# Attention scores in 32x64 tiles straight from the queries, without a masked copy, and new instruction orders

## The chip, the cores and the metric

The kernel runs on one core of one Trainium2 chip. The metric is the device time of one execution in microseconds (us). An engine is named as the profile names it: PE is TensorE's matmul stream and PEld its weight loads, DVE is VectorE, ACT ScalarE, POOL GpSimd and SP SyncE, which issues transfers.

## The reference

Four layers on 2048 tokens of 448 features, attention and a gated product in turn (A, B, A, B, the weights used twice). Attention has 16 heads of 28 features; each token looks at 8 keys: itself and every second token before it.

```python
def _A_ref(x, wqkv, wo):                      # H = 16, Dh = 28
    W, dil = 8, 2
    qkv = ((x @ wqkv).reshape(B, S, 3, H, Dh)).transpose(2, 0, 3, 1, 4)
    q, k, v = qkv[0], qkv[1], qkv[2]
    idx = pos[:, None] - (jnp.arange(W) * dil)[None, :]
    mask = idx >= 0
...
    logits = jnp.einsum("bhsd,bhswd->bhsw", q, kg) * Dh ** -0.5
    logits = jnp.where(mask[None, None, :, :], logits, -1e9)
    o = jnp.einsum("bhsw,bhswd->bhsd", _softmax(logits, axis=-1), vg)
    return o.transpose(0, 2, 1, 3).reshape(B, S, D) @ wo

def _B_ref(x, w_gate, w_up, w_down):
    h = (x @ w_gate) * (x @ w_up)
    return h @ w_down

x = x + _A_ref(_layernorm(x), A_wqkv, A_wo)
x = x + _B_ref(_layernorm(x), B_w_gate, B_w_up, B_w_down)
x = x + _A_ref(_layernorm(x), A_wqkv, A_wo)
x = x + _B_ref(_layernorm(x), B_w_gate, B_w_up, B_w_down)
```

## The kernel before

Everything stays on the chip between the layers: `x_sb` holds the tokens, `xnTa` and `xnTb` their normalised transposes, `qk` the keys (plane 0) and queries (plane 1), `hT` the gated product. The even tokens come first and the odd ones behind them, two halves of 1024, so that the eight keys of a token are its neighbours in the row.

**TensorE in tiles.** A matmul can use part of the 128x128 array, and several such tiles work beside each other. The projections, the gate and up products and the down product run as pairs in two tiles of 64 rows by 128 columns (L355 in `pair`, 64 features in each). The attention uses smaller tiles. A head has 28 features, and in `qk` four heads stand on the four groups of 32 partitions. Each attention layer has nine groups of queries: the first is one block of 128 queries, the others are two blocks of 120 each. For a group, `attn_front` computes the scores of all 16 heads (the score burst, L855, into four banks of PSUM), ScalarE takes their exponent into `E_sb` (L864), VectorE masks them with a minimum (L871); `attn_back` multiplies with the values (the output burst, L889, tiles of 64 rows by 32 columns) and collects the result in a slot of `O_sb`, where it waits for its normalisation.

**The masked queries.** A score tile before has 64 rows, so it holds the keys of two heads. To keep their scores apart, VectorE writes the group's queries twice into `Qz`, once with every odd head zeroed and once with every even one (L841, `qmask`). One matmul then gives the scores of both heads, side by side. In the groups of `WIDE_S` (the first six of the first layer) the tiles are 64x64, 32 matmuls to a group; in the other twelve they are 64x32, 64 matmuls to a group, each over 64 or 80 columns. The first group of a layer has half as many.

**Strips.** A score or output burst can be cut at places given in the order, and there a step of another product is put in. That step, a pair of 64x128 matmuls, is then issued as eight strips of 64x32 (L358 in `pair`, `alt_of`): the same tile shape that output bursts and narrow score bursts have. The 64x64 bursts are not cut.

**What sets the order.** Nothing is decided at run time. `ORDER` lists for each engine the operations by number, each with the places of its cuts and the hosts of its strips, and `BANKS` gives the PSUM banks of every TensorE operation; `emit` turns dependencies into semaphore waits. Some evictions can go to ScalarE or VectorE, and `ORDER` decides which.

Of the kernel before, what the change touches and what calls it, by code (L numbers as in the profile page):

```python
# [30 lines left out]
WIDE_S = ((0, 0), (0, 1), (0, 2), (0, 3), (0, 4), (0, 5))  # L31
# [16 lines left out]
NO = 4  # L48
NE_ = 2
NR_ = 2  # L50
NZ = 1
# [46 lines left out]
def grp_nc(g):  # L98
# [21 lines left out]
    ),  # L120
    "act": (
# [224 lines left out]
def pe_cols(n):  # L346
    return n / 2.4 + 2.6
# [36 lines left out]
def build(nc, A_x, A_wqkv, A_wo, B_w_gate, B_w_up, B_w_down, out):  # L384
# [35 lines left out]
    Qz = sb([128, NZ, 2, 4, 2 * QB], bf, "Qz")  # L420
    qmask = sb([128, 2], dt.float32, "qmask")
    hT = sb([128, FC, 2, 512], bf, "hT")
    oT = sb([128, 4, HALF], bf, "oT")
# [18 lines left out]
    def one(fn, key=None):  # L442
        return [(fn, key)]
# [718 lines left out]
```

## Time and profile before

| | before |
|---|---|
| median of 3 runs | 379.52 us (379.1 to 379.61) |
| profiled execution | 380.59 us, of which the span from the first to the last instruction is 378.9 us |
| PE busy | 373.2 us (99%) |
| PEld busy | 208.2 us (55%) |
| DVE busy | 271.6 us (72%) |
| ACT busy | 199.3 us (53%) |
| POOL busy | 5.2 us (1%) |
| score bursts on PE (L855) | 912 matmuls: 736 in 64x32 tiles, 176 in 64x64 |
| output bursts on PE (L889) | 1088 matmuls in 64x32 tiles |
| strips on PE (L358) | 560 matmuls in 64x32 tiles |

A matmul's busy time is modelled: the next ones start while it is still shown as running, so neighbours overlap, and the time that a group takes is read from the start of the next group rather than from the sum of durations. A row of the order of time gives the start, the time to the last end, and the number of equal instructions.

### The profile page before, as it was taken

To read this page: it belongs to the slowest core of one execution; us is meant where nothing else is said; L and a number is where in the kernel's file an instruction comes from. 1 tells how busy PE (TensorE), PEld (TensorE's weight loads), DVE (VectorE), ACT (ScalarE), POOL (GpSimd) and SP (SyncE) were. 2 spreads that over 40 slices of the span, in tenths; PEclk is the share of its full clock that TensorE was granted. 3 is DMA by queue.
4 is the path that set the end of the run, shared out by engine and by line. 5 is a ranking of instruction groups with operands and counts; after the bars stand their busy time and mean duration, and the time that the engine had idled before them with its cause. 6 is when DMAs were issued, how large, how long until landed. Compare 5 with 4: busy or idle time off the path is not lost.

```text
span 378.9 us, 14223 instructions
## 1 busy us (share of the span) xinstructions
PE 373.2 (99%) x6372; PEld 208.2 (55%) x6372; DVE 271.6 (72%) x564; ACT 199.3 (53%) x333; POOL 5.2 (1%) x25
## 2 busy tenths in 40 slices
PE   8999999999999999999999999999999999999997
PEld 3554678544544445455766756554455454444864
DVE  6999989988786385867477978528897587275233
ACT  4898786657444565444466413556766544123310
POOL 5000000000000000000000000000000000000000
DMA  7767464610414023022102125220026104103002
GB/s 248 179 139 150 55 185 132 111 23 21 82 22 69 5 55 72 20 48 55 24 10 52 39 43 100 49 51 21 20 32 95 39 3 90 44 2 74 2 13 98
DMA packets 59892, 24.38 MB, mean 64 GB/s; under 512 B 49016, under 2 KB 59704, under 8 KB 59832
## 3 DMA queue, kind: packets, MB, share of 16 engines
q1 hardware_dynamic: 59688, 23.42, 29.0%
q8 instruction: 50, 0.82, 0.9%
q14 instruction: 10, 0.08, 0.1%
q10 hardware_dynamic: 144, 0.06, 0.1%
HBM read 9.04 MB, written 3.50 MB: 33 GB/s over the span
## 4 chain that ended last, share of the span: by engine, by line
PE 92%; ACT 4%; DMA 2%; SPq 1%; DVE 1%; issue 0%; DVEq 0%
PE ps L355 84%; PE ps L358 4%; PE ps L855 2%; ACT qk L730 2%; PE ps L889 2%; DMA hT<-in_A_wqkv_dram 2%; PE ps L1031 1%; SPq L450 1%; ACT E_sb L864 1%; ACT v_sb L822 0%; ACT R_sb L919 0%; ACT R_sb L920 0%; ACT O_sb L900 0%; DVE WQK L517 0%; DVE Qz L841 0%
## 5 line engine op out<-in xcount | busy, mean ns | idle before, releaser
L355 PE MATMUL ps<-xnTb,WGU 64*128 64x512 bf16 (+1 forms) x1902 | 171.6, 332 | 0.8 <-ACT R_sb L920 0.8
L355 PEld LDWEIGHTS ps<-xnTb,WGU 64*128 64x128 bf16 x1902 | 92.2, 94 | 70.3 <-issue 1.5
L1013 ACT ACTIVATE g_sb<-ps 128x512 bf16<-128x512 f32 x112 | 65.8, 596 | 90.7 <-PE ps L355 86.4
L1019 DVE TENSOR_TENSOR hT<-g_sb,ps 128x512 bf16<-128x512 bf16 x112 | 75.1, 681 | 40.1 <-ACT g_sb L1013 38.8
L355 PE MATMUL ps<-WD,hT 64*128 64x448 bf16 x786 | 80.5, 349 | 0.0
L980 DVE TENSOR_TENSOR x_sb<-x_sb,ps 128x448 bf16<-128x448 bf16 x62 | 36.3, 615 | 30.1 <-PE ps L355 29.8
L355 PEld LDWEIGHTS ps<-WD,hT 64*128 64x128 bf16 x786 | 37.7, 94 | 33.7 <-DVE hT L1019 0.2
L355 PE MATMUL ps<-xnTa,WQK 64*128 64x512 bf16 (+1 forms) x496 | 52.6, 353 | 0.5 <-DVE WQK L517 0.2
L864 ACT ACTIVATE E_sb<-ps,shift_sb 128x1024 bf16<-128x1024 f32 (+1 forms) x36 | 37.2, 1068 | 11.7 <-PE ps L855 11.7
L592 DVE BATCH_NORM_STATS2 st<-x_sb 128x6 f32<-128x448 bf16 x64 | 38.2, 618 | 1.4 <-DMA x_sb<-in_A_x_dram 1.2
L355 PEld LDWEIGHTS ps<-xnTa,WQK 64*128 64x128 bf16 x496 | 22.7, 94 | 22.6 <-DVE O_sb L904 1.0
L730 ACT ACTIVATE qk<-ps 128x1024 bf16<-128x1024 f32 (+1 forms) x28 | 25.4, 931 | 17.5 <-PE ps L355 17.1
L616 DVE TENSOR_SCALAR xn_sb<-x_sb,mv,rstd 128x512 bf16<-128x512 bf16 (+1 forms) x64 | 27.6, 455 | 4.9 <-ACT rstd L597 4.9
L871 DVE TENSOR_TENSOR E_sb<-E_sb,MK 128x1024 bf16<-128x1024 bf16 (+1 forms) x36 | 23.4, 658 | 9.0 <-ACT E_sb L864 8.9
L355 PE MATMUL ps<-wo_g,oT 64*128 64x448 bf16 x151 | 26.0, 350 | 0.0
L355 PE MATMUL ps<-WV,xnTa 64*128 64x336 bf16 (+3 forms) x244 | 23.6, 304 | 0.4 <-DMA WV<-in_A_wqkv_dram 0.4
L919 ACT ACTIVATE R_sb<-R_sb 128x960 f32<-128x960 f32 (+1 forms) x18 | 17.3, 961 | 11.4 <-DVE R_sb L918 11.4
L918 DVE STREAM_SHUFFLE R_sb<-O_sb 128x960 f32<-128x960 f32 (+1 forms) x18 | 21.2, 1180 | 0.0
L900 ACT ACTIVATE O_sb<-ps 128x448 f32<-128x448 f32 (+2 forms) x27 | 13.9, 548 | 11.5 <-PE ps L889 11.3
L939 DVE TENSOR_TENSOR oT<-O_sb,R_sb 128x960 bf16<-128x960 f32 (+1 forms) x16 | 17.5, 1095 | 3.2 <-ACT R_sb L920 3.2
L595 ACT ACTIVATE lnv<-mv,eps_sb 128x2 f32<-128x2 f32 (+1 forms) x33 | 9.2, 292 | 20.0 <-DVE mv L594 17.7
L920 ACT ACTIVATE R_sb<-R_sb 128x960 f32<-128x960 f32 (+1 forms) x18 | 17.3, 959 | 0.3
(67 smaller groups left out, 243.2 us busy)
## 6 DMA issues: line engine op xcount, KB each, us to landing
out_dram<-x_sb SPq DMA_DIRECT2D x15, 112.0 KB, 1.8
x_sb<-in_A_x_dram SPq DMA_DIRECT2D x3, 448.0 KB, 7.4
hT<-in_A_wqkv_dram SPq DMA_DIRECT2D x4, 224.0 KB, 5.5
WGU<-in_B_w_gate_dram SPq DMA_DIRECT2D x4, 224.0 KB, 4.1
WGU<-in_B_w_up_dram SPq DMA_DIRECT2D x4, 224.0 KB, 3.8
WD<-in_B_w_down_dram SPq DMA_DIRECT2D x2, 448.0 KB, 4.2
mv_rows<-oT SPq DMA_DIRECT2D x12, 64.0 KB, 1.7
oT<-mv_rows SPq DMA_DIRECT2D x48, 8.0 KB
```

What stands on the lines that cost most here:

```text
L355: return lambda E: E.matmul(out(), lhs(), rhs(), start=start, stop=stop)
L592: sc.add("dve", one(lambda E, B=B: E.bn_stats(st6[:, B, :], x_sb[:, B, :]), ("bn", li, B)), 525.0, deps=[("x", li - 1, B)] + ([("xn", li - ...
L616: sc.add("dve", one(lambda E, B=B, dst=dst, src=src: E.tensor_scalar(dst, src, mv[:, B, 0:1], rstd[:, B:B + 1], ALU.subtract, ALU.mult), ( ...
L730: return E.activation(dst, src, ACT.Copy) if hasattr(E, "activation") else E.tensor_copy(dst, src)
L864: return E.activation(E_sb[:, slot, 2 * hp:2 * hp + 2, 0:w], ps[:, b0:b0 + 2, 0:w], ACT.Exp, bias=shift_sb[:, 0:1], scale=SCALE)
L871: return E.tensor_tensor(e, e, MK[:, kind, 0:nc].unsqueeze(1).unsqueeze(1).to_broadcast([128, 2, w // nc, nc]), ALU.min)
L918: sc.add("dve", one(lambda E: E.stream_shuffle(R, Of, [DH] * 32), ("Rs", li, qb)), dve_est(w) + 20.0, deps=[("Oa", li, g)] + prev, prio=prio)
L919: sc.add("act", one(lambda E: E.activation(R, R, ACT.Ln), ("Rl", li, qb)), act_est(w, False), deps=[("Rs", li, qb)], prio=prio)
L939: return E.tensor_tensor(dst, O.rearrange("p d h n -> p h d n"), Rv.rearrange("p d h n -> p h d n"), ALU.mult)
L980: sc.add("dve", one(lambda E: E.tensor_tensor(x_sb[:, B, :], x_sb[:, B, :], ps[:, bk[w], 0:D], ALU.add), ("x", li, B)), dve_est(D), deps=[ ...
L1013: sc.add("act", one(lambda E, gs=gs, bk=bk: E.activation(g_sb[:, gs, :], ps[:, bk[0], :], ACT.Copy), ("G", li, j, f0)), act_est(512), deps ...
L1019: return E.tensor_tensor(hT[:, f0:f0 + nf, hs, 0:nt], v(g_sb[:, gs, :]), v(ps[:, bk[1], :]), ALU.mult)
```

## The change

The score tile becomes 32 rows by 64 columns. Each matmul takes the 28 rows of one head, unmasked, from `qk`: 64 keys against 64 queries. The four heads of a row group pattern go to four PSUM banks, and eight tiles (four groups of rows, two of columns) can work at once. All groups have this form, `WIDE_S` is gone, and with it `Qz`, `qmask` and the 36 masking instructions. A group of two blocks now has 64 matmuls in every case, of 64 columns each. `E_sb` is laid out by head, which changes the addresses that the minimum and the output burst read; the group that lies across the two halves takes its minimum in two parts. `O_sb` gets six slots for four.

```diff
-WIDE_S = ((0, 0), (0, 1), (0, 2), (0, 3), (0, 4), (0, 5))
+SCORES = "C32"
-NO = 4
+NO = 6
-NZ = 1
...
 ORDER = {
     "pe": (
-        "41 42 43 44 45 46 47 48 49 50 51 52 53 54 112 115 55 56 57 58 211 130 212 133 139 241 136 242 205 235 206 236 229 201 230 203 231 202 157 232 199 154 "
+        "39 40 41 42 43 44 45 46 47 48 49 50 51 52 110 113 53 54 55 56 209 128 131 210 134 238 137 239 199 203 200 204 232 226 233 155 228 227 152 229 201 197 "
...
-        zs, zprev = ring("z", ("S", li, qbs[-1]))
-        def fz(E, a):
-            return E.tensor_scalar(Qz[:, zs, a, :, 0:end - tok], qk[:, 1, :, tok:end], qmask[:, a:a + 1], None, ALU.mult)
-        sc.add("dve", [((lambda E, a=a: fz(E, a)), ("Qz", li, g) if a else None) for a in range(2)], 2 * (4 * (end - tok) * 0.33 + 62.0), deps=qdeps + [zprev, "c_qm"], prio=prio)
...
-        wide = (li, g) in WIDE_S
-        KN = 64 if wide else 32
-        for hc, d, c, s_, p in [(hc, d, c, s_, p) for hc in range(4) for d in range(nd) for s_ in range(64 // KN) for c in range(2) for p in range(2)]:
+        for hc, d, c, r in [(hc, d, c, r) for hc in range(4) for d in range(nd) for c in range(2) for r in range(4)]:
             ck, nk, cq, nq = qb_info(qbs[d])
-            ks, qs = ck + 64 * c + KN * s_, cq + 56 * c - tok
-            b, h = e_at(nd, hc, d, p)
-            lo, hi = max(0, ks - qs - tok), min(nc, ks - qs - tok + KN + W)
-            ins.append((lambda E, hc=hc, c=c, s_=s_, p=p, b=b, h=h, ks=ks, qs=qs, lo=lo, hi=hi: E.matmul(
-                ps[64 * c + KN * s_:64 * c + KN * s_ + KN, bk[b], 2 * nc * h:2 * nc * (h + 1)].rearrange("p (a n) -> p a n", a=2)[:, :, lo:hi], qk[64 * p:64 * p + 64, 0, hc, ks:ks + KN],
-                Qz[64 * p:64 * p + 64, zs, :, hc, qs + lo:qs + hi], start=True, stop=True, tile_position=(64 * p, 64 * c + KN * s_)), None))
+            ks, qs, o = ck + 64 * c, cq + 56 * c, (d * 4 + hc) * nc
+            lo, hi = max(0, ks - qs), min(nc, ks - qs + 64 + W)
+            ins.append((lambda E, hc=hc, c=c, r=r, ks=ks, qs=qs, o=o, lo=lo, hi=hi: E.matmul(
+                ps[64 * c:64 * c + 64, bk[r], o + lo:o + hi], qk[32 * r:32 * r + DH, 0, hc, ks:ks + 64], qk[32 * r:32 * r + DH, 1, hc, qs + lo:qs + hi],
+                start=True, stop=True, tile_position=(32 * r, 64 * c)), None))
...
-        sc.add("pe", ins, sum(pe_cols(2 * n) for n in cols) / (4 if wide else 8), deps=deps + [prev, ("Qz", li, g)], mode="C64" if wide else BURST, acquire=bk, prio=prio)
+        sc.add("pe", ins, sum(pe_cols(n) for n in cols) / 8, deps=deps + [prev], mode=SCORES, acquire=bk, prio=prio)
...
-            sc.add("dve", one(fm, ("E", li, g, hp)), dve_est(2 * w, 2.0, 60.0), deps=[("Ex", li, g, hp), f"c_mk{kind}"], prio=prio)
+            sc.add("dve", [((lambda E, hp=hp, p=p: fm(E, hp, *p)), ("E", li, g, hp) if p is parts[-1] else None) for p in parts], dve_est(2 * w, 2.0, 60.0 * len(parts)),
+                   deps=[("Ex", li, g, hp)] + [f"c_mk{k}" for k in sorted(set(kinds))], prio=prio)
```

The strips keep their shape. After the change ten of the 18 score bursts are cut, nine of them three times and one twice; before, ten were cut, three times each. In the changed kernel L354 stands for L355, L357 for L358, L838 for L855, L873 for L889.

First place: PE, the ninth group of the first layer, whose score burst is cut in both kernels by strips of the gate and up products. `32x2x40` is an output of 32 partitions and 80 columns (a 64x32 tile with two heads), `64x64` one of 64 partitions (a 32x64 tile). Before:

```order
L855 MATMUL ps<-Qz,qk 32x2x32 x2
L855 MATMUL ps<-Qz,qk 32x2x40 x4
L855 MATMUL ps<-Qz,qk 32x2x32 x4
L855 MATMUL ps<-Qz,qk 32x2x40 x4
L855 MATMUL ps<-Qz,qk 32x2x32 x2
L358 MATMUL ps<-xnTb,WGU 32x512 x8
L855 MATMUL ps<-Qz,qk 32x2x32 x2
```

And after the change:

```order
L838 MATMUL ps<-qk 64x64 x16
L357 MATMUL ps<-xnTb,WGU 32x512 x8
L838 MATMUL ps<-qk 64x64 x16
L357 MATMUL ps<-xnTb,WGU 32x512 x8
L838 MATMUL ps<-qk 64x64 x8
L357 MATMUL ps<-xnTb,WGU 32x512 x8
L838 MATMUL ps<-qk 64x64 x24
```

The cuts stand after the same numbers of matmuls (16, 16 and 8), and the strips between them have another tile shape than the scores now.

Second place: PE, early in the first layer, where score bursts stand whole between projections. Before, the third group:

```order
L889 MATMUL ps<-E_sb,v_sb 32x64 x64
L355 MATMUL ps<-xnTa,WQK 128x512 x42
L855 MATMUL ps<-Qz,qk 64x128 x32
L355 MATMUL ps<-xnTa,WQK 128x256 x14
L355 MATMUL ps<-xnTa,WQK 128x512 x6
```

After the change:

```order
L354 MATMUL ps<-xnTa,WQK 128x256 x6
L354 MATMUL ps<-xnTa,WQK 128x512 x8
L354 MATMUL ps<-xnTa,WQK 128x256 x8
L838 MATMUL ps<-qk 64x64 x64
L354 MATMUL ps<-wo_g,oT 128x448 x8
```

Where 32 matmuls of 128 columns stood are 64 of 64 columns.

Third place: DVE at the same stage, with the eviction of queries and keys (L730, then L725), the mask copies (L841) and the minimum (L871, then L855). Before:

```order
L841 TENSOR_SCALAR Qz<-qk,qmask 128x960 x2
L795 CAST v_sb<-ps 128x8x28
L939 TENSOR_TENSOR oT<-O_sb,R_sb 128x4x128
L904 TENSOR_TENSOR O_sb<-O_sb,ps 128x8x8
L918 STREAM_SHUFFLE R_sb<-O_sb 128x960
L730 CAST qk<-ps 128x2x512 x2
```

After the change:

```order
L790 CAST v_sb<-ps 128x8x28
L923 TENSOR_TENSOR oT<-O_sb,R_sb 128x4x128
L884 COPY O_sb<-ps 128x8x56
L888 TENSOR_TENSOR O_sb<-O_sb,ps 128x8x8
L902 STREAM_SHUFFLE R_sb<-O_sb 128x960
L725 CAST qk<-ps 128x2x512
```

The mask copies are gone, and an eviction of outputs (L884) that ScalarE did stands in their stead. Over the whole program VectorE now does 12 evictions of queries and keys instead of 8 and 14 of outputs instead of 9, and ScalarE as many fewer.

More of the change, by code (lines that the diff above doesn't have):

```diff
@@ L503, in build @@
     memset("pool", ones32, 1.0, "c_ones", 100)
-    sc.add("dve", one(lambda E: E.memset(qmask[:], 0.0), "i_qm"), 60, prio=-39.5)
-    sc.add("dve", [((lambda E, r=r: E.memset(qmask[32 * r:32 * r + DH, r % 2:r % 2 + 1], 1.0)), "c_qm" if r == 3 else None) for r in range(4)], 240, deps=["i_qm"], prio=-39.5)
     wb = Banks(1)
@@ L562, in build @@
     WO = [("wp", w, b) for w in range(2) for b in range(4)] + [("wp", 2, 0), ("wp", 2, 1)] + [("wo", j) for j in range(4)]
[L564 removed]
+    rings = {n: [None] * k for n, k in (("xn", NXN), ("o", NO), ("v", NV), ("v2", NV2), ("e", NE if PAIRED else 2 * NE), ("r", NR), ("g", NG))}
     rpos = {n: 0 for n in rings}
@@ L836, in attn_front @@
         k0, tok, end = qb_info(qbs[0])[0], qb_info(qbs[0])[2], sum(qb_info(qbs[-1])[2:])
-        qdeps = [("QK", li, j, c) for j in chunks_of(li, tok, end) for c in range(4)]
         deps = [("QK", li, j, c) for j in chunks_of(li, k0, end) for c in range(4)]
-        zs, zprev = ring("z", ("S", li, qbs[-1]))
-        def fz(E, a):
-            return E.tensor_scalar(Qz[:, zs, a, :, 0:end - tok], qk[:, 1, :, tok:end], qmask[:, a:a + 1], None, ALU.mult)
-        sc.add("dve", [((lambda E, a=a: fz(E, a)), ("Qz", li, g) if a else None) for a in range(2)], 2 * (4 * (end - tok) * 0.33 + 62.0), deps=qdeps + [zprev, "c_qm"], prio=prio)
         slot, prev = ring("e", ("AV", li, qbs[-1]))
@@ L866, in attn_front, with fm @@
         for hp in range(2):
[L867 to L872 removed]
+            kinds = [0 if q == 0 else 2 if q == STRADDLE else 1 for q in qbs]
+            parts = [(0, nd, kinds[0])] if len(set(kinds)) == 1 else [(d, d + 1, kinds[d]) for d in range(nd)]
+            def fm(E, hp, a, z, kind):
+                e = E_sb[:, slot, 2 * hp:2 * hp + 2, 4 * a * nc:4 * z * nc].rearrange("p b (m n) -> p b m n", n=nc)
+                return E.tensor_tensor(e, e, MK[:, kind, 0:nc].unsqueeze(1).unsqueeze(1).to_broadcast([128, 2, 4 * (z - a), nc]), ALU.min)
+            sc.add("dve", [((lambda E, hp=hp, p=p: fm(E, hp, *p)), ("E", li, g, hp) if p is parts[-1] else None) for p in parts], dve_est(2 * w, 2.0, 60.0 * len(parts)),
+                   deps=[("Ex", li, g, hp)] + [f"c_mk{k}" for k in sorted(set(kinds))], prio=prio)
         return slot
@@ L886, in attn_back @@
             vw = v_sb[64 * c:64 * c + 64, vslot[q], 32 * h:32 * h + 32] if t < 0 else v2_sb[64 * c:64 * c + 64, v2slot[q], 32 * t:32 * t + 32]
-            eb, eh = e_at(nd, hc, d, b // 2)
-            eo = (2 * eh + b % 2) * nc
-            ins.append((lambda E, b=b, c=c, o=o, vw=vw, eb=eb, eo=eo: E.matmul(ps[32 * b:32 * b + 32, bk[c], o:o + nc], vw, E_sb[64 * c:64 * c + 64, slot, eb, eo:eo + nc],
+            eo = (d * 4 + hc) * nc
+            ins.append((lambda E, b=b, c=c, o=o, vw=vw, eo=eo: E.matmul(ps[32 * b:32 * b + 32, bk[c], o:o + nc], vw, E_sb[64 * c:64 * c + 64, slot, b, eo:eo + nc],
                                                                start=True, stop=True, tile_position=(64 * c, 32 * b)), None))
```

10 lines of the change are left out of this document (removed), and 112 rows, old and new, of tables (BANKS, ORDER).

## The prediction

> **What bounds the kernel now.** I read the page first, then the busy time by stretch, then the waits of TensorE, and last the order of time inside single bursts.
>
> ```profile
> PE 373.2 (99%) x6372; PEld 208.2 (55%) x6372; DVE 271.6 (72%) x564; ACT 199.3 (53%) x333; POOL 5.2 (1%) x25
> PE   8999999999999999999999999999999999999997
> PE 92%; ACT 4%; DMA 2%; SPq 1%; DVE 1%; issue 0%; DVEq 0%
> ```
>
> TensorE is busy in every slice, and 92% of the chain that ended last is its own. A busy PE need not be at its peak, so the next views ask whether it ever stands still.
>
> ```profile
> 0.00:20.00 20.00, 18.09 (x204) 9.42 (x206) 16.65 (x59) 12.86 (x30) 5.20 (x25) 1.00 0.73 203
> 20.00:60.00 40.00, 38.73 (x846) 24.60 (x844) 36.60 (x80) 34.67 (x53) 0.00 (x0) 1.00 0.64 143
> 60.00:300.00 240.00, 239.93 (x4420) 131.77 (x4416) 178.92 (x355) 128.57 (x209) 0.00 (x0) 1.00 0.25 48
> ...
> PE ps L509 <- DVE hT L480: 1.2, 1, 1.2
> PE ps L355 <- ACT R_sb L920: 0.8, 1, 0.8
> PE ps L355 <- DMA WV<-in_A_wqkv_dram: 0.4, 1, 0.4
> PE ps L355 <- DVE WQK L517: 0.2, 1, 0.2
> ```
>
> The stretches list time, then PE, PEld, DVE, ACT and POOL busy, the granted clock (1.00 throughout) and DMA. From 60 to 300 us TensorE has 0.07 us of idle time in 240, while VectorE and ScalarE have 61 and 111 us to spare. There, a nanosecond added to TensorE's stream is a nanosecond of the kernel, and one taken from VectorE is nothing. Only from 20 to 60 us do three engines share the limit: PE 38.73, DVE 36.60, ACT 34.67 of 40. So the change is priced on TensorE, burst by burst.
>
> **The change on TensorE: what a burst costs now.** Here is the order of time on PE around four bursts, then the means by shape (rows of lines by form; "64*32" is tile rows by tile columns).
>
> ```profile
> 23.67 0.59 PE L355 MATMUL ps<-xnTa,WQK 64*128 64x512 bf16 x4
> 24.20 0.64 PE L855 MATMUL ps<-Qz,qk 64*64 64x128 bf16 x32
> 24.77 0.60 PE L355 MATMUL ps<-xnTa,WQK 64*128 64x512 bf16 x3
> ...
> 80.06 0.59 PE L355 MATMUL ps<-xnTb,WGU 64*128 64x512 bf16 x4
> 80.59 0.25 PE L889 MATMUL ps<-E_sb,v_sb 64*32 64x64 bf16 x16
> 80.66 0.40 PE L358 MATMUL ps<-xnTb,WGU 64*32 64x512 bf16 x8
> 80.87 0.24 PE L889 MATMUL ps<-E_sb,v_sb 64*32 64x64 bf16 x16
> 80.93 0.40 PE L358 MATMUL ps<-xnTb,WGU 64*32 64x512 bf16 x8
> 81.14 0.21 PE L889 MATMUL ps<-E_sb,v_sb 64*32 64x64 bf16 x8
> 81.17 0.40 PE L358 MATMUL ps<-xnTb,WGU 64*32 64x512 bf16 x8
> 81.39 0.27 PE L889 MATMUL ps<-E_sb,v_sb 64*32 64x64 bf16 x24
> 81.59 0.39 PE L355 MATMUL ps<-xnTb,WGU 64*128 64x512 bf16 x2
> ...
> 117.88 0.26 PE L855 MATMUL ps<-Qz,qk 64*32 64x64 bf16 x16
> ...
> 118.94 0.60 PE L355 MATMUL ps<-xnTb,WGU 64*128 64x512 bf16 x4
> ...
> 197.99 0.68 PE L855 MATMUL ps<-Qz,qk 64*32 64x64 bf16 x64
> 198.60 0.61 PE L355 MATMUL ps<-xnTb,WGU 64*128 64x256 bf16 x8
> ```
>
> ```profile
> L355 PE MATMUL ps<-xnTa,WQK 64*128 64x512 bf16 x384 | 46.4, 377 | 0.2
> L355 PE MATMUL ps<-WD,hT 64*128 64x448 bf16 x786 | 80.5, 349 | 0.0
> L855 PE MATMUL ps<-Qz,qk 64*64 64x128 bf16 x168 | 3.6, 219 | 0.0
> ```
>
> *Price of a change of tile shape.* The four big matmuls at 80.06 are two pairs. A single one lasts 0.377, so the second pair started 0.59 - 0.377 = 0.21 us after the first; that is the time a pair streams. Two pairs take 0.43, yet the short burst begins 0.53 after 80.06: 0.10 us is lost at the change from 64x128 tiles to 64x32. At 23.67 the change to 64x64 costs the same (24.20 - 23.67 - 0.43). On the way out, the last of the 32 matmuls started at 24.20 + 0.64 - 0.219 = 24.62 and streams about 0.05 (32 of them, four at a time, in 0.42); the next pair comes at 24.77: 0.10 again.
>
> *No change of shape, no price.* Strips (L358, big matmuls cut into 64x32 tiles) and the short matmuls of the attention outputs have one shape. A round of eight strips takes 80.87 - 80.66 = 0.21 and 81.39 - 81.17 = 0.22 us, which is what a pair of the same columns takes uncut. Strips inside a burst are free.
>
> *What the new order adds.* The changed scores use 32x64 tiles; the strips stay at 64x32. Ten of the 18 score bursts are cut by strips, nine of them three times and one twice: 29 cuts. Before, all cuts were within one shape. Now each is a change in and a change out, 58 in all. Outside the cuts there were 70 changes (68 between big matmuls and bursts, two where an output burst met a score burst of 64x64 directly) and are now 71 (70 and one). With two more at the program's ends the count goes from 72 to 131: 59 more. At 0.10 us: **+5.9 us**. No row shows 32x64 meeting 64x32. The bounds are 0 (the strip rounds above) and 0.10. I take 0.10, since in this program every meeting of two shapes pays it, whether the columns alone change (64x128 to 64x32 and to 64x64) or the rows alone. For the rows, the end of the program:
>
> ```profile
> 370.31 0.73 PE L355 MATMUL ps<-WD,hT 64*128 64x448 bf16 x6
> 370.97 0.55 PE L1031 MATMUL ps<-WD,hT 128*128 128x448 bf16 x2
> ```
>
> Three pairs of 448 columns begin 0.19 us apart ((0.73 - 0.35)/2, by the 0.35 us that one such matmul lasts), the third at 370.69; it streams until 370.88, and the 128x128 tile comes at 370.97: 0.09 us. A change of both is nearer to these than to no change.
>
> [...]
>
> *The bursts themselves.* Less their exit (0.10), an uncut group of 32 at 64x64 takes 24.77 - 24.20 - 0.10 = 0.47; an uncut group of 64 at 64x32 takes 198.60 - 197.99 - 0.10 = 0.51; a cut score burst, less three rounds of strips, 118.94 - 117.88 - 0.65 - 0.10 = 0.31; a cut output burst, whose 64 matmuls have the 64 columns that the new scores have, 81.59 - 80.59 - 0.65 - 0.10 = 0.25 (0.65 is three rounds at 0.216). Before: 5 x 0.47 + 10 x 0.31 + 0.51, and the two groups of half size taken at half (0.24 and 0.26): 6.5 us. After: 6 x 0.51 + 10 x 0.25, and two halves at 0.26: 6.1 us. **-0.4 us**. Half the columns per matmul in the wide groups buys nothing, because there are twice as many matmuls.
>
> *Weight loads.* They double to 64 columns, all hidden behind the stream in my sum:
>
> ```profile
> L855 PEld LDWEIGHTS ps<-Qz,qk 64*32 64x32 bf16 x736 | 9.2, 90 | 5.8 <-issue 2.9 <-DVE hT L1019 0.9 <-DVE xn_sb L616 0.4
> L855 PEld LDWEIGHTS ps<-Qz,qk 64*64 64x64 bf16 x176 | 2.7, 106 | 2.0 <-issue 0.8 <-ACT rstd L597 0.6 <-ACT g_sb L1013 0.4
> ```
>
> A load of 64 columns is 16 ns longer than one of 32, and eight run beside each other. If the cover is gone, a tile may take a new load only as fast as the wide groups show, every 0.47/8 = 0.059 us instead of the 0.031 of a round at 0.25/8: 80 rounds x 0.028 = +2.2 us. This is a rival below.
>
> **The change on the other engines.**
>
> ```profile
> L841 DVE TENSOR_SCALAR Qz<-qk,qmask 128x960 bf16<-128x960 bf16 x32 | 13.5, 464 | 2.5 <-ACT qk L730 2.5
> L841 DVE TENSOR_SCALAR Qz<-qk,qmask 128x512 bf16<-128x512 bf16 x4 | 1.2, 353 | 0.3 <-ACT qk L730 0.3
> L730 ACT ACTIVATE qk<-ps 128x1024 bf16<-128x1024 f32 x22 | 22.2, 1022 | 17.3 <-PE ps L355 17.1
> L730 DVE CAST qk<-ps 128x1024 bf16<-128x1024 f32 x6 | 7.3, 1214 | 0.0
> ...
> 48.60 0.64 PE L855 MATMUL ps<-Qz,qk 64*64 64x128 bf16 x32
> 50.05 0.40 PE L355 MATMUL ps<-xnTb,WGU 64*128 64x256 bf16 x4 [0.81 <-ACT R_sb L920]
> ```
>
> The masked copies, 14.7 us of VectorE, go, and the new order hands VectorE evictions that ScalarE did (two more 1024-wide QK evictions at 1.21 us against 1.02 on ScalarE, five more of the attention outputs). From 60 us on both are covered by TensorE: nothing. Before that, the front is worth something: the burst at 48.60 is followed after 1.45 us where its like took 0.57, a wait of 0.88 us, and PE's idle time from 20 to 60 us is 1.27. The bounds are 0 and -2 us (that idle, and some more under modelled ends); lighter ScalarE and VectorE should take part of it, and the scores no longer wait for a mask (0.93 us for a group's two). I take **-0.8 us**. What is late next there is the QK eviction itself, which the scores still need. The masking minimum is split in two for the group that straddles the two token halves (four instructions more over the two layers, on VectorE, covered as above). Two more slots for outputs let an output burst start before older ones are normalised; no row of TensorE's waits names such a slot, so nothing. The queue of SP issues the same transfers in another order, and the chain names none of them between 20 us and the last output.
>
> **The sum**: 5.9 - 0.4 - 0.8 = +4.7 us. The profiled execution took 380.59 us for a span of 378.9, so it should become a span of 383.6 and 385.3 us. The median of the runs is 379.52, lower by 1.07; on it the forecast is **384.2 us**.
>
> **Rivals.**
>
> *No drain between 32x64 and 64x32 tiles.* Then the 5.9 us fall to the 0.1 of one change and the change is worth -0.4 - 0.8: 378.3 us, from 377.3 to 379.3. For it speaks that strips and short matmuls of one shape flow without a gap; against it stand the three pairs of shapes above, each with its 0.09 to 0.10. It decides as soon as a change costs under 1.2/59 = 0.020 us.
>
> *Weight loads come through.* 384.2 + 2.2 = 386.4 us. For it: the scores' loads are twice as wide and each tile gets one every 0.03 us, which no row shows; against it, 16 ns more of duration is little. [...]
>
> *Cheaper changes or a fuller gain in front.* A change at 0.06 us, or all 2 us of the front's waits: 381 to 382.5 us.
>
> **How the numbers follow.** Full drain, 382.5 to 386: 0.64. Weight loads on top, 386 to 388: 0.08. The cheaper case, 380.5 to 382.5: 0.10. No drain: 0.18, of which 0.11 lies under 378.76. A change within 0.2% (378.76 to 380.28) is about what a measurement of this kernel cannot tell from none. So faster 0.11, same 0.07, slower 0.82. The range from 380.5 to 387.5 holds the first three but for the end of the second, 0.81.
>
> **What would show it.** In the changed kernel's order of time, strips should begin 0.09 to 0.10 us later than the stream of the scores ahead of them allows, and scores the same after strips; a round of strips inside a score burst should take 0.31 us, not 0.21, with the outputs' bursts as before. PE's idle time from 60 to 300 us stays near nothing while the span grows. If the rounds inside score bursts stay at 0.21, the forecast is wrong and the first rival right; if eight scores take 0.06, the second.

## The result: 389.88 us, slower, and by twice what was forecast

| | before | after |
|---|---|---|
| median | 379.4 us (379.1 to 379.61, 4 runs) | 389.88 us (389.76 to 390.49, 4 runs) |
| ratio to before | | 1.028, 95% interval 1.0262 to 1.0298 |
| profiled execution, its span | 380.59 us, 378.9 us | 390.49 us, 388.8 us |

The direction was right and the size was not: +4.7 us was forecast, +10.5 came by the medians (+9.9 between the two profiled executions), and 389.88 lies above the range. The page of the changed kernel, its busy engines and its chain:

```profile
PE 381.6 (98%) x6518; PEld 209.7 (54%) x6518; DVE 266.2 (68%) x536; ACT 194.8 (50%) x324; POOL 5.1 (1%) x25
PE 94%; ACT 2%; DMA 2%; DVE 1%; issue 1%; DVEq 0%
```

TensorE is still the chain. Its busy time grew by 8.4 us, while VectorE lost 5.4, which bought nothing. The same stretches as before the change, and TensorE's longest waits:

```profile
20.00:60.00 40.00, 37.42 (x996) 23.45 (x994) 32.32 (x66) 32.77 (x48) 0.00 (x0) 1.00 0.55 126
60.00:300.00 240.00, 239.03 (x4236) 129.43 (x4232) 170.38 (x335) 119.37 (x196) 0.00 (x0) 1.00 0.26 48
...
PE ps L354 <- DMA xnTb<-xn_sb: 1.6, 1, 1.6
PE ps L504 <- DVE hT L477: 1.2, 1, 1.2
PE ps L354 <- issue: 0.9, 1, 0.9
```

From 20 to 60 us PE is busy for 37.42 us instead of 38.73: the lighter VectorE and ScalarE (32.32 and 32.77 busy, from 36.60 and 34.67) did not become less waiting but more. From 60 to 300 us there is almost 1 us of idle time where there was 0.07, and it is one wait, put down to "issue", which is to say to nothing that the profile shows. The clock is 1.00 throughout.

The order of time on PE in a cut score burst, the counterpart of the burst at 117.88 before:

```profile
121.70 0.27 PE L838 MATMUL ps<-qk 28*64 28x64 bf16 x16
121.90 0.41 PE L357 MATMUL ps<-xnTb,WGU 64*32 64x512 bf16 x8
122.24 0.27 PE L838 MATMUL ps<-qk 28*64 28x64 bf16 x16
122.43 0.41 PE L357 MATMUL ps<-xnTb,WGU 64*32 64x512 bf16 x8
122.77 0.23 PE L838 MATMUL ps<-qk 28*64 28x64 bf16 x8
122.94 0.41 PE L357 MATMUL ps<-xnTb,WGU 64*32 64x512 bf16 x8
123.28 0.30 PE L838 MATMUL ps<-qk 28*64 28x64 bf16 x24
123.51 0.60 PE L354 MATMUL ps<-xnTb,WGU 64*128 64x512 bf16 x4
...
204.07 0.71 PE L838 MATMUL ps<-qk 28*64 28x64 bf16 x64
204.71 0.94 PE L354 MATMUL ps<-xnTb,WGU 64*128 64x256 bf16 x14
```

(The profile writes the 32x64 tile as 28*64, by the 28 rows that are used.) A round of eight strips inside a score burst takes 122.24 - 121.90 = 0.34 us, where it took 0.21, and sixteen scores ahead of strips take 0.20 instead of 0.07. The whole burst lasts 123.51 - 121.70 = 1.81 us, of which three rounds of strips stream 0.64 (at the pace of uncut pairs, 0.213 us for 512 columns): 1.17 us for the scores. Before, the burst at 117.88 took 118.94 - 117.88 - 0.64 = 0.42.

To see where all of the time is, I took the start of every matmul from the traces and counted each burst so, from its first matmul to the next big one, less its strips' own stream (a wait begins where the next matmul would have started):

| us | score bursts | output bursts | waits of PE | rest | first to last matmul |
|---|---|---|---|---|---|
| before | 8.45 | 7.72 | 3.44 | 355.36 | 374.97 |
| after | 15.80 | 7.95 | 5.38 | 355.73 | 384.86 |
| difference | +7.35 | +0.23 | +1.94 | +0.37 | +9.89 |

The split depends a little on where a wait is taken to begin. With the idle time of PE that the profile shows as the waits (3.24 and 4.80 us), the four differences are +7.50, +0.27, +1.56 and +0.56.

So two things are to be explained: score bursts that cost 7.35 us more (forecast: +5.5), and waits that cost 1.94 us more (forecast: 0.8 less). The theory for the first is the forecast's, a price for each change of tile shape, dearer than 0.10; its rivals are the width of the weight loads, the rows of the tile as such, and the number of short matmuls in a row. For the second it is the new order, or something that the profile does not name.

### The profile page after: what moved, and what is told of

The parts are those of the page before. It is cut to its first block, busy times and chain, and to the rows that moved or that the text cites. A ratio compares the mean times of both kernels' runs of the same rounds, so it can differ in the third digit from the quotient of the medians.

```text
span 388.8 us, 14482 instructions
## 1 busy us (share of the span) xinstructions
PE 381.6 (98%) x6518; PEld 209.7 (54%) x6518; DVE 266.2 (68%) x536; ACT 194.8 (50%) x324; POOL 5.1 (1%) x25
## 4 chain that ended last, share of the span: by engine, by line
PE 94%; ACT 2%; DMA 2%; DVE 1%; issue 1%; DVEq 0%
PE ps L354 82%; PE ps L357 4%; PE ps L838 3%; PE ps L504 2%; DMA xnTb<-xn_sb 2%; PE ps L873 2%; PE ps L1015 1%; ACT qk L725 1%; PE ps L630 0%; DVE R_sb L902 0%; DVE oT L923 0%; ACT R_sb L904 0%; ACT R_sb L903 0%; ACT O_sb L884 0%; DVE O_sb L884 0%
## 5 line engine op out<-in xcount | busy, mean ns | idle before, releaser
L354 PE MATMUL ps<-xnTb,WGU 64*128 64x512 bf16 (+1 forms) x1908 | 172.1, 332 | 1.6 <-DMA xnTb<-xn_sb 1.6
L354 PEld LDWEIGHTS ps<-xnTb,WGU 64*128 64x128 bf16 x1908 | 92.3, 94 | 71.1 <-issue 2.5
L1003 DVE TENSOR_TENSOR hT<-g_sb,ps 128x512 bf16<-128x512 bf16 x112 | 75.5, 681 | 54.5 <-ACT g_sb L997 52.7
L354 PE MATMUL ps<-WD,hT 64*128 64x448 bf16 x790 | 80.6, 349 | 0.9 <-issue 0.9
L354 PEld LDWEIGHTS ps<-WD,hT 64*128 64x128 bf16 x790 | 38.2, 94 | 35.0 <-issue 1.7
L354 PE MATMUL ps<-xnTa,WQK 64*128 64x512 bf16 (+1 forms) x496 | 52.0, 352 | 0.4 <-DVE WQK L520 0.2
L354 PEld LDWEIGHTS ps<-xnTa,WQK 64*128 64x128 bf16 x496 | 23.2, 94 | 22.4 <-DVE xnTa L640 1.0
L855 DVE TENSOR_TENSOR E_sb<-E_sb,MK 128x1024 bf16<-128x1024 bf16 (+2 forms) x40 | 23.6, 606 | 7.0 <-ACT E_sb L847 7.0
L725 ACT ACTIVATE qk<-ps 128x1024 bf16<-128x1024 f32 (+1 forms) x24 | 22.5, 948 | 11.3 <-PE ps L354 11.0
L354 PE MATMUL ps<-wo_g,oT 64*128 64x448 bf16 x154 | 26.3, 350 | 0.4 <-DVE oT L923 0.4
L354 PE MATMUL ps<-WV,xnTa 64*128 64x336 bf16 (+3 forms) x242 | 23.6, 305 | 0.0
L884 ACT ACTIVATE O_sb<-ps 128x512 f32<-128x512 f32 (+3 forms) x22 | 11.5, 557 | 13.5 <-PE ps L873 13.5
L838 PEld LDWEIGHTS ps<-qk 28*64 28x64 bf16 x1088 | 10.2, 103 | 12.6 <-issue 9.6
```

Source lines behind the costliest of these rows:

```text
L354: return lambda E: E.matmul(out(), lhs(), rhs(), start=start, stop=stop)
L725: return E.activation(dst, src, ACT.Copy) if hasattr(E, "activation") else E.tensor_copy(dst, src)
L838: ins.append((lambda E, hc=hc, c=c, r=r, ks=ks, qs=qs, o=o, lo=lo, hi=hi: E.matmul(ps[64 * c:64 * c + 64, bk[r], o + lo:o + hi], qk[32 * r ...
L855: return E.tensor_tensor(e, e, MK[:, kind, 0:nc].unsqueeze(1).unsqueeze(1).to_broadcast([128, 2, 4 * (z - a), nc]), ALU.min)
L1003: return E.tensor_tensor(hT[:, f0:f0 + nf, hs, 0:nt], v(g_sb[:, gs, :]), v(ps[:, bk[1], :]), ALU.mult)
```

## Experiments

All times are medians, and all ratios are to the kernel before on the same chip (379.5 to 380.3 us).

**1. No cuts in the score bursts.** The changed kernel; the hosts of the strips follow their burst whole.

```diff
-495*3.5/468:1+311:1
+495 468 311
-543*2.4.5/405:3
+543 405
... (and eight more)
```

> The changed kernel with no cut in a score burst: the ten cut bursts stand whole and their strips are issued as ordinary pairs behind them; all else as changed. Theory A (58 changes of tile shape at the cuts cost about 0.125 us each): a cut burst takes 1.16 us beside its strips, a whole one 0.64, so ten of them give 5.2 us back: 389.9 - 5.2 = 384.7 us, with the waits outside the bursts as in the changed kernel. Rival B (the new score tiles are slow in themselves, by their weight loads or the new places of the operations, and the cuts cost no more than strips of the old shape did): less than 1.5 us back, 388.4 us or more.

385.19 us (384.59 to 386.17), ratio 1.0098 (1.0065 to 1.0132): theory A's size. Without any cut the 58 changes are gone, and the score bursts fall from 15.80 to 10.87 us.

```profile
119.94 0.72 PE L826 MATMUL ps<-qk 28*64 28x64 bf16 x64
120.59 1.69 PE L342 MATMUL ps<-xnTb,WGU 64*128 64x512 bf16 x14
```

An uncut burst takes 0.65 us (0.64 as a mean), so the scores alone, with no strips between, cost more than a cut burst of before, 0.42. The gain from the cuts' removal is 15.80 - 10.87 = 4.93 us over 58 changes, 0.085 each: less than the 0.125 that theory A gives a change, so something is lost with the cuts; experiment 5 shows what.

**2. The new tile shape in the old order.** The kernel before, its masked copies still made but not read; the scores come from `qk` in 32x64 tiles as in the changed kernel.

```diff
-            b, h = e_at(nd, hc, d, p)
-                Qz[64 * p:64 * p + 64, zs, :, hc, qs + lo:qs + hi], ..., tile_position=(64 * p, 64 * c + KN * s_)), None))
+                ps[64 * c:64 * c + 64, bk[r], o + lo:o + hi], qk[32 * r:32 * r + DH, 0, hc, ks:ks + 64], qk[32 * r:32 * r + DH, 1, hc, qs + lo:qs + hi],
+                start=True, stop=True, tile_position=(32 * r, 64 * c)), None))
```

> The kernel before, its orders, its four output slots and its masked copies (still written, now read by nobody), with the new score tiles alone: 32x64, straight from the queries. Theory A: 30 cuts, 60 changes of shape at 0.125 = 7.5 us, and five whole groups at 0.64 for 0.57 us: 379.4 + 7.5 + 0.4 = 387.3 us; the waits stay at the 3.4 us of the kernel before. Rival C (at least half of the loss comes with the new orders, not with the tiles): 384 us or less.

392.23 us (390.56 to 393.47), ratio 1.028 (1.023 to 1.0331): slower than expected. Its cut bursts take 1.17 us like those of the changed kernel, so the shape and not the order makes the price. What comes on top is not in the bursts' changes but in stops, and most of it in one place:

```profile
48.77 0.59 PE L853 MATMUL ps<-qk 28*64 28x64 bf16 x47
51.06 0.34 PE L853 MATMUL ps<-qk 28*64 28x64 bf16 x17 [1.70 <-issue]
```

TensorE stops in the middle of a score burst, 17 matmuls from its end, and waits for nothing that the profile names. Two shorter stops of the same kind stand at 24.94 (0.65 us) and at 208.24 (0.39). Experiment 7 takes them up, and the last section what follows the longest.

**3. The old tile shape in the new order.** The changed kernel with score tiles of 64 rows by 32 columns, straight from the unmasked queries.

```diff
-                ps[64 * c:64 * c + 64, bk[r], o + lo:o + hi], qk[32 * r:32 * r + DH, 0, hc, ks:ks + 64], qk[32 * r:32 * r + DH, 1, hc, qs + lo:qs + hi],
-                start=True, stop=True, tile_position=(32 * r, 64 * c)), None))
+                qk[64 * p:64 * p + 64, 0, hc, ks:ks + 32],
+                qk[64 * p:64 * p + 64, 1, hc, qs + lo:qs + hi].unsqueeze(1).to_broadcast([64, 2, hi - lo]), start=True, stop=True, tile_position=(64 * p, 64 * c + 32 * s_)), None))
```

> The changed kernel, its orders and six slots, with score tiles of 64 rows by 32 columns again, but without a mask: the scores of two heads are mixed, which the time does not see. Left out: the masking. Theory A: no change of shape at a cut, 58 x 0.125 = 7.3 us less: 382.6 us; what stays above the 379.4 before are waits of the new orders, about 2 us, and some 0.5 us of whole bursts. Rival C: the loss is with the orders, 385 us or more. If even the front's waits go, 380.5 us or less.

384.32 us (381.74 to 385.75), ratio 1.0086 (1.0059 to 1.0113): 5.6 us less than the changed kernel with the same orders and no masks, and the ratio is lower by 1.9 points. As a time it lies between theory A's 382.6 and rival C's 385; PE stands idle for 5.48 us here, more than in the changed kernel (4.80), and part of that is in stops of experiment 7's kind. The bursts decide. The one that stands at 121.70 there, first and last rows:

```profile
121.06 0.26 PE L839 MATMUL ps<-qk 64*32 64x64 bf16 x16
121.13 0.41 PE L357 MATMUL ps<-xnTb,WGU 64*32 64x512 bf16 x8
121.34 0.26 PE L839 MATMUL ps<-qk 64*32 64x64 bf16 x14
...
121.86 0.32 PE L839 MATMUL ps<-qk 64*32 64x64 bf16 x24
122.11 1.04 PE L354 MATMUL ps<-xnTb,WGU 64*128 64x512 bf16 x8
```

0.21 us for a round of strips and 1.05 for the burst, as before. The same cuts at the same places are free where the shapes agree; with 32x64 tiles they cost 1.168 - 0.414 = 0.754 us, over six changes 0.126 each. The orders, the cuts and the strips are the same in both; the scores differ in tile shape, and with it in weights loaded (32 columns instead of 64) and in columns streamed (64 to 80 instead of 64). Standing whole, the two shapes cost nearly the same (0.615 and 0.64 us), so it is the meeting with the strips that makes the price.

**4. No masked copies.** The kernel before with the mask copies shrunk to one column; the scores mix two heads.

```diff
-            return E.tensor_scalar(Qz[:, zs, a, :, 0:end - tok], qk[:, 1, :, tok:end], qmask[:, a:a + 1], None, ALU.mult)
+            return E.tensor_scalar(Qz[:, zs, a, 0, 0:1], qk[:, 1, 0, tok:tok + 1], qmask[:, a:a + 1], None, ALU.mult)
...
-                Qz[64 * p:64 * p + 64, zs, :, hc, qs + lo:qs + hi], ...
+                qk[64 * p:64 * p + 64, 1, hc, tok + qs + lo:tok + qs + hi].unsqueeze(1).to_broadcast([64, 2, hi - lo]), ...
```

> The kernel before with its orders and tiles, but the masked copies shrunk to one column and the scores read from the unmasked queries: heads are mixed, the time of 14.5 us of VectorE is left out. The forecast had put 0.8 us on a lighter front: 378.6 us. Theory D (VectorE's work is covered nearly everywhere, and what the front waits for is not VectorE): 379.0 to 379.5 us.

379.76 us (378.77 to 381.09), ratio 0.9977 (0.9955 to 1.0). VectorE's 14.7 us of masks are worth at most 0.45% of the time. In the trace PE's idle time falls from 3.24 to 2.54 us, but all except 0.1 us of that lies in the first 20 us, ahead of the first masked copy (at 20.67 us in the kernel before). From 20 to 60 us, where the forecast had looked for its gain, the idle time goes from 1.27 to 1.18 us.

**5. One cut instead of three.** The changed kernel.

```diff
-495*3.5/468:1+311:1
+495*4/468:1 311
-543*2.4.5/405:3
+543*4/405:1
... (and eight more)
```

> The changed kernel with a single cut in each of its ten cut score bursts instead of three or two: 10 strip rounds stay, 20 of the 58 changes between scores and strips. Theory A (a cut costs two changes of shape, 0.25 us together, and gives part of it back, since an uninterrupted run of short matmuls slows down after the first rounds): a burst less its strips' own stream takes about 0.64 us, as uncut (0.638), against 1.17 with three cuts; the sum of score bursts comes to about 11 us, as without any cut (10.87), and the time to 385 us. Theory B (only the number of changes counts, at 0.126 each, and an uncut burst's 0.64 is a burst's own work): 0.64 + 0.25 = 0.89 us a burst, score bursts about 13.4 us, and 387.5 us.

386.56 us (385.33 to 388.13), ratio 1.0175 (1.0143 to 1.0207). The span of the profiled run, 383.6 us, is 0.8 longer than without cuts; the medians differ by 1.4, so the time alone lies between the theories' 385 and 387.5. The bursts tell them apart:

```profile
120.16 0.33 PE L826 MATMUL ps<-qk 28*64 28x64 bf16 x32
120.42 0.42 PE L345 MATMUL ps<-xnTb,WGU 64*32 64x512 bf16 x8
120.77 0.33 PE L826 MATMUL ps<-qk 28*64 28x64 bf16 x32
121.03 1.04 PE L342 MATMUL ps<-xnTb,WGU 64*128 64x512 bf16 x8
```

121.03 - 120.16 - 0.21 = 0.66 us a burst (0.659 to 0.677 over the ten): theory A of the two, against 0.89 by theory B. The first cut costs two changes and gives back nearly as much. The reason shows in the pieces: 32 matmuls up to the strips take 0.26 us with the change in it, but 64 in one go take 0.65; a long run of short matmuls slows down after its first rounds, in both shapes. In an uncut burst the first four rounds of eight start within 0.12 us, the fifth 0.12 us after the fourth, and the later ones 0.067 us apart; a piece between two strips is too short to get there. (Before, the 64 of 64x32 at 197.99 take 0.61 uncut and 0.41 cut three times.) So cuts by strips are worth about 0.2 us to a burst, and this worth was part of every cut before. Why a long run slows down no run shows.

**6. The price of a change by itself.** The kernel before; the fourth of the seven steps of 84 products is issued as eight strips. (Twelve of the 84 are halves of the down product, with 448 columns instead of 512.)

```diff
+                elif e == "pe" and len(got) == 1 and got[0].alt and len(got[0].alt) > 3 and got[0].acquire is not None and got[0].acquire.kind == 1 and len(got[0].ins) == 14:
+                    o = got[0]
+                    seq = [(o, n) for n in range(6)] + [(o, o.alt[3][q]) for q in range(8)] + [(o, n) for n in range(8, 14)]
```

> The kernel before, with the fourth of the seven steps of 84 gate and up products (512 columns, the ones that host no strips) issued as eight strips of 64x32 instead of a pair of 64x128: 168 more changes of tile shape, each between matmuls of 512 columns, with no short matmul near. Theory A (the drain alone is 0.094 to 0.103 us, and the rest of the 0.126 found per change in the score bursts comes from the short matmuls' own first rounds): +16 to +17 us, 396 us. Theory B (a change costs 0.126 us whatever stands on its sides): +21 us, 400.6 us. Theory C (strips themselves, hidden so far, cost nothing and a drain is partly covered by 512 columns): under +14 us.

399.04 us (398.91 to 400.26), ratio 1.05 (1.047 to 1.053): +19.5 us for 168 changes, 0.116 each, between theory A (0.10) and theory B (0.126).

```profile
150.50 0.73 PE L358 MATMUL ps<-WD,hT 64*128 64x448 bf16 x6
151.16 0.38 PE L361 MATMUL ps<-WD,hT 64*32 64x448 bf16 x8
151.48 0.74 PE L358 MATMUL ps<-WD,hT 64*128 64x448 bf16 x6
```

Three pairs of 448 columns stream 0.56 us and the strips come after 0.66; the strips stream 0.187 and the next pair comes after 0.32. Over all 84 places, alike within 3 ns: about 93 ns on the way into the strips and 128 on the way out, from the first strip, as the eight strips start over 23 ns and the next pair comes 105 ns later than the stream of the last of them alone would ask. The pair behind that is some 10 ns late as well. A round of strips costs 0.227 to 0.231 us in all, by the pace that is given to an uncut pair; 0.227 is used below. The forecast took the way out to be as dear as the way in and left the 23 ns out. The remaining 0.126 - 0.1135 = 0.012 per change goes with the short matmuls themselves: the first round of eight scores after strips takes 52 ns, the next ones 32, and 20 ns to two changes is near it.

**7. Another 112 instructions ahead of everything.** The changed kernel; eight warm-up matmuls as eight of 64 columns each.

```diff
-    ... one(lambda E, n=n: E.matmul(ps[:, n % NBK if n < NBK else wb[0], :], warm[:, 0:128], warm, start=True, stop=True), ("warm", n)), 427.0
+    return lambda E: E.matmul(ps[:, n % NBK if n < NBK else wb[0], 64 * i:64 * i + 64], warm[:, 0:128], warm[:, 64 * i:64 * i + 64], start=True, stop=True)
+    ... [(fw(n, i), ("warm", n) if i == 7 else None) for i in range(8)] if n < 8 else one(...)
```

> The changed kernel with eight of its warm-up matmuls, which compute nothing that is used, issued as eight of 64 columns each instead of one of 512: 112 more instructions on TensorE ahead of all work, the same order behind. Theory A (TensorE's unexplained idle times, 1.07 us near 70.7 in the changed kernel and 1.9 near 49 in the version with the orders of before, are waits for the next 256 instructions of 64 bytes, whose count in the trace is 193 more than a multiple of 256): the idle time near 70.7 goes from that matmul, and whatever idle time of PE over 0.3 us is put down to nothing lies where the recounted number of instructions is again 193 more than a multiple of 256; the time falls by up to 1 us or, if another boundary meets dense work, stays. Theory B (the idle time belongs to that matmul, a wait the profile does not show): it stays at the same matmul, 112 instructions later in the count.

392.31 us (391.14 to 392.92), ratio 1.032 (1.0294 to 1.0345): not faster, slower. But the places tell the theories apart. In the changed kernel, around the wait for "issue", and at the same work here:

```profile
70.35 0.73 PE L354 MATMUL ps<-WD,hT 64*128 64x448 bf16 x5
71.98 0.91 PE L354 MATMUL ps<-WD,hT 64*128 64x448 bf16 x7 [0.90 <-issue]
```

```profile
72.57 1.30 PE L354 MATMUL ps<-WD,hT 64*128 64x448 bf16 x12
...
52.26 1.15 PE L354 MATMUL ps<-xnTb,WGU 64*128 64x256 bf16 x18
54.71 0.39 PE L354 MATMUL ps<-xnTb,WGU 64*128 64x256 bf16 x4 [1.31 <-issue]
```

The twelve matmuls of the down product now run through, and a new wait of 1.31 us has come up inside a gate and up product that ran through before. (The time is not these stops alone: a wait of 1.21 us for ScalarE's eviction of values at 69.61 is new, and the wait of 1.57 us for `xnTb` is gone, since `xnTb` landed at 49.11 us instead of 49.88. PE's idle time is 6.02 us in all, against 4.80.) Counting all of PE's records (matmuls, weight loads, and the semaphore waits that no view counts as busy) up to each stop over half a microsecond from start to start that is put down to "issue":

| kernel | records up to the stop | stop, from start to start | remainder by 256 |
|---|---|---|---|
| after | 3009 | 1.25 us | 193 |
| 2 (shape, old order) | 705, 1985, 7617 | 0.85, 1.91, 0.58 | 193, 193, 193 |
| 3 (64x32, new order) | 705, 3009, 7617 | 0.71, 1.42, 0.53 | 193, 193, 193 |
| 5 (one cut) | 705, 3009, 7361 | 0.63, 0.92, 0.60 | 193, 193, 193 |
| 7 (112 more) | 961, 2241, 7617 | 0.81, 1.57, 0.85 | 193, 193, 193 |
| 9 (below) | 705 | 0.70 | 193 |
| 1, 3, 5, at one place near 48.5 us | 1883, 1887, 1883 | 0.68, 0.71, 0.73 | 91, 95, 91 |
| before, 4, 6, 8 | none | | |

Fourteen stand at the same place of a 256-instruction piece, and the place in the work moved with the 112 instructions. The other three are a kind of their own: they stand in the last matmuls of the output burst just ahead of the wait for `xnTb`, 7 to 11 records before it; their cause is open, and as the product behind them waits for `xnTb` anyway, they cost little. The transfers agree: queue q8 moved 51 pieces of 16 KB in the changed kernel's run (the row lists pieces, MB and share).

```profile
q8 instruction: 51, 0.84, 0.9%
```

In the changed kernel one ran from 69.30 to 70.54 us, and the stop is from 70.73 to 71.98; in this one, from 52.11 to 53.23 and from 53.14 to 54.71. With 13,171 records in all, 51 pieces are one for each 256. The traces also tell when such a stop comes. Number the places with remainder 193 and the pieces in order: the second place goes with the first piece, and so on. All fourteen stops end 1.25 to 1.65 us after their piece has landed. At the 521 places of the eleven traces that TensorE reaches 1.7 us or more after the landing, no matmul comes over 0.32 us behind the one before it. (Fifteen other places within 1.65 us have a shorter stop or none.) In the kernel before the shortest such distance is 1.75 us, and it has no stop. How many pieces TensorE holds at a time no run shows. Most pieces come in time (50 of 51 in the changed kernel, all in the one before), and why some come late is open: the stops stand in or shortly behind bursts, but other pieces that are used up as fast come in time. So theory A holds, with its less welcome end: a shift moves the stops and does not remove them.

**8. The burst back ahead of the wait, first form.** In the changed kernel's order the score burst of the eighth pair of blocks had moved behind the gate and up product that waits for `xnTb`. Here it goes back.

```diff
-... 337 346 289 358 292 ...
+... 337 346 358 289 292 ...
```

> The changed kernel with one move in its order: the score burst of the first layer's eighth pair of blocks goes ahead of the gate and up product that waits for xnTb (near 48 us), where before had it; PSUM banks of seven operations are renamed for it, and one exponent on ScalarE goes ahead of one eviction. Theory A (the transposed tokens come at the same time, 50.0 to 50.2 us, whatever TensorE does before, so the burst fills the wait): the idle time there falls from 1.6 to about 0.9 us and the time by 0.6 to 0.8 us, to 389.2. Theory B (the wait follows the burst, because ScalarE or VectorE then have more to do ahead of the transpose's source): no change, 389.9 us.

391.45 us (389.16 to 393.19), ratio 1.0292 (1.0258 to 1.0327): inconclusive, because the renamed banks made waits of their own, and the runs fall into two groups. Four have a mean granted clock of 0.995 or 0.996 and take 391.4 to 393.19 us; two have 1.00 and take 389.16 and 389.25 (the last section shows two traces with such a drop).

```profile
48.13 0.68 PE L873 MATMUL ps<-E_sb,v_sb 64*32 64x64 bf16 x64 [0.41 <-ACT qk L725]
48.73 1.04 PE L838 MATMUL ps<-qk 28*64 28x64 bf16 x64
50.83 1.38 PE L354 MATMUL ps<-xnTb,WGU 64*128 64x256 bf16 x22 [1.05 <-DVE v_sb L817]
```

The product now waits for VectorE's eviction of values from the bank that it was given, and the output burst for an eviction of keys. These two waits are 1.46 us, nearly the 1.57 that the move was to shorten. That the profiled run still meets theory A's 389.2 is luck: it has no stop for instructions near 70.7, and the move was not made for that.

**9. The same move without these waits.** The banks of all later operations are exchanged in a ring, and VectorE evicts the values first.

```diff
-... 337 346 289 358 292 ...   (pe)
+... 337 346 358 289 292 ...
-... 525 348 349 338 275 ...   (dve)
+... 525 338 348 349 275 ...
-289:45 292:67 ... 358:0123 ...   (banks; all later ones likewise, 01 to 23, 23 to 45, 45 to 67, 67 to 01)
+289:67 292:01 ... 358:2345 ...
```

> The changed kernel with the same move as in e5_front (the score burst of the eighth pair of blocks ahead of the gate and up product that waits near 48 us), now without new waits of its own: the PSUM banks of everything from there on are exchanged in a ring, so that the output burst and the product keep banks that are free as early as in the changed kernel, and VectorE evicts the values ahead of the two instructions on the outputs. Theory A (the product waits for xnTb alone, which comes at 49.9 to 50.2 us whatever TensorE does before): the wait ahead of the product falls from 1.46 us to about 0.85, as in before, and the time by 0.6 us, to 389.2, unless a wait for instructions arises elsewhere, since 256-instruction pieces now end at other work. Theory B (the wait follows the burst): the product starts 0.6 us later, the time stays at 389.9.

392.09 us (391.15 to 392.44), ratio 1.0315 (1.0293 to 1.0337): right at its place and wrong in the time. The place first, in the changed kernel and here:

```profile
47.97 0.68 PE L873 MATMUL ps<-E_sb,v_sb 64*32 64x64 bf16 x64
50.22 1.71 PE L354 MATMUL ps<-xnTb,WGU 64*128 64x256 bf16 x28 [1.57 <-DMA xnTb<-xn_sb]
```

```profile
48.17 0.68 PE L873 MATMUL ps<-E_sb,v_sb 64*32 64x64 bf16 x64
48.78 1.06 PE L838 MATMUL ps<-qk 28*64 28x64 bf16 x64
50.09 3.23 PE L354 MATMUL ps<-xnTb,WGU 64*128 64x256 bf16 x56 [0.24 <-DVE O_sb L884]
...
62.56 0.94 PE L354 MATMUL ps<-wo_g,oT 64*128 64x448 bf16 x8
65.77 0.28 PE L873 MATMUL ps<-E_sb,v_sb 64*32 64x64 bf16 x24 [2.28 <-DVE st L587]
```

The product starts at 50.09 instead of 50.22 with the whole burst done ahead of it; the wait fell from 1.57 to 0.24 us. `xnTb` lands at 49.84 us here and at 49.88 in the changed kernel, so the move left its arrival alone (theory A). Thirteen microseconds later an output burst waits 2.28 us, where the changed kernel had no wait, and that takes all of it back, with slower matmuls behind it (last section). The instruction named there is statistics of another layer's tokens, on which the burst does not depend. Of what it does depend on, the transposed values come late: the transfer issued at 60.21 us lands at 65.68, and the burst's first weights are loaded at 65.74. In the changed kernel the same transfer was issued at 59.15 and landed at 62.55, ahead of the burst at 64.33. That fits a wait for it, but no run was made to test it. The number of records there, 2562, is 2 more than a multiple of 256, so it is not one of the stops at remainder 193.

## Why the forecast was right in direction and wrong in size

*The drain.* Shown as a price: strips inside 32x64 scores pay, 0.126 us a change, strips inside 64x32 scores in the same order do not (experiment 3), and strips between big matmuls pay too, 0.1135 us a change (experiment 6). So the rival without a drain falls. In the prediction and the expectations the word stands for the time that a change takes, which is what the runs show; what TensorE does in that time they do not show.

*The count.* 59 more changes was right: the matmuls' shapes in the traces change 72 times before and 131 times after.

*The price of a change, 0.10 us: the first step that failed.* It was read as the same in and out. Alone it is 0.1135 (experiment 6), in the score bursts 0.126 (experiment 3). For the 58 changes at the cuts that is 58 x 0.126 = 7.3 us instead of 5.8.

*The bursts themselves, -0.4 us: failed.* A cut score burst was given the 0.25 us of a cut output burst (the one at 80.59, among the shortest: 0.37 us with its exit, where most take 0.39). Without its changes it measures 1.168 - 3 x 0.227 - 0.105 = 0.38 (0.105 for the exit). Part of that is the 0.012 per change above. The halves and whole groups came out near the forecast: 0.64 with the exit, against 0.61. Together, 7.35 us stand against the 5.5 that these steps made of it (5.9 - 0.4): 1.9 us of the miss.

*The front, -0.8 us: failed, in sign.* Lighter engines were to shorten the waits. Experiment 4 gives the whole worth of the masks there: 0.1 us of idle time from 20 to 60 us. And the new order took the score burst that had filled part of the wait for `xnTb` and put it behind: in both kernels the product begins near 50.1 us (50.05 and 50.22), but before there was a burst more done by then. That is 0.77 us more of waiting by the starts of the matmuls, and experiment 9 shows that the move back closes it there. I had the row of that wait before me (48.60 and 50.05) and read it as a wait to be shortened by other engines, not as one whose length depends on what TensorE still has to do ahead of it.

*What had no step: the supply of instructions.* 1.07 us at 70.73 (1.25 from start to start, less 0.19 for the pair under way). No row of before shows such a stop, and the forecast looked at engines and transfers of data only. These two waits make 1.84 of the 1.94 us; with the 0.8 that did not come, 2.7 us of the miss. The remaining 0.6, in output bursts and between big matmuls, stays unexplained, and so does the 0.5 us by which the medians lie farther apart than the profiled executions.

*Weight loads coming through.* Not shown, and the pieces speak against it: the second and third rounds of eight scores take 32 ns each with loads of 64 columns and 29 in 64x32 tiles with loads of 32, the late rounds of uncut bursts take 67 ns in both, and uncut bursts as a whole differ by 0.64 - 0.615 = 0.02 us. That its time, 386.4, was nearer than the forecast's is chance.

*More evictions on VectorE, six slots for outputs, the queue of transfers: nothing.* From 60 us on the only wait of the changed kernel over 0.3 us is that for instructions, so these cost nothing there.

No run beats the kernel before. The changed kernel without cuts or with one comes within 1 to 2%, and the masks, which were to be saved, are worth less than a measurement can tell.

## What to carry to other kernels

Count the changes of tile shape that a new shape causes with its neighbours, strips included, and price a round trip at 0.23 us here, from first start to next start and not from one end; cuts by strips of the same shape are not only free but gain a burst 0.2 us here, because a long run of short matmuls slowed down (rounds of eight 0.03 us apart up to the fourth and 0.067 from the fifth on). Read a wait at a fixed arrival by what work stands ahead of it: the order that moved work behind the wait lengthened it by 0.77 us here, and the one that moved it back woke another of 2.28 us behind (experiment 9). A stop that the profile puts down to "issue" is worth a count of the instructions ahead of it, and a look at when the last piece of instructions landed, before a cause is sought in the data.

## What the hardware showed that was not expected

TensorE stops where the profile shows only "issue": 0.5 to 1.9 us from start to start, fourteen of seventeen at one place of a piece of 256. In all fourteen, matmuls go on 1.25 to 1.65 us after a piece has landed.

Two long stops cost more than themselves. Behind the 2.28 us in experiment 9 TensorE has a granted clock of 0.50 for about 3.4 us:

```profile
66.40:67.00 0.60, 0.60 (x36) 0.38 (x22) 0.00 (x0) 0.12 (x1) 0.00 (x0) 0.50 0.00 0
...
69.00:69.60 0.60, 0.60 (x10) 0.41 (x8) 0.00 (x0) 0.00 (x0) 0.00 (x0) 0.50 0.38 97
69.60:70.20 0.60, 0.60 (x12) 0.48 (x10) 0.00 (x0) 0.19 (x1) 0.00 (x0) 0.97 0.12 27
```

Fourteen pairs of 256 columns took 2.8 us there, 1.3 more than usual. Behind the 1.70 us in experiment 2 it is the same, a mean granted clock of 0.61 from 51.0 to 51.4 us and of 0.50 from there to 54.5, and 1.6 us lost, which is a third of that run's distance from its expectation; the 1.31 us in experiment 7 and the 1.57 us of the changed kernel left the clock at 1.00. Half speed for 3.4 of 390 us makes a mean of 0.996, and runs of one kernel differ in it: three of four in experiment 2, one of four in experiment 5, four of six in experiment 8 and two of five in experiment 9 have 0.995 or 0.996. What sets the clock down and up again no run shows.
